# Issuing the output stores of an attention and FFN kernel from ScalarE's queue instead of SyncE's

## The chip, the cores and the metric

The kernel runs on one core of one Trainium2 chip. The metric is the device time of one execution in microseconds (us); before the change it is 480.43 us at the median of 3 runs (480.08 to 480.87). Busy times, waits and the places of single instructions come from one profiled execution, whose clock starts at the first recorded instruction.

A core has five engines, each with an instruction queue that it works off in order: TensorE (PE) multiplies matrices, VectorE (DVE) and ScalarE (ACT) work on elements, GpSimd (POOL) issues most loads here, SyncE (SP) only issues DMAs. Engines wait for one another by semaphores.

## What is computed

Attention with a projected key and value length (64 instead of 1024), for 8 batches and 8 heads, and then a feed-forward network on its result.

```python
k_proj = einsum('ks,bhsd->bhkd', E, k)             # 8 x 8 x 64 x 64
v_proj = einsum('ks,bhsd->bhkd', F, v)
attn   = softmax(q @ k_proj.T / 8)                 # q: 8 x 8 x 1024 x 64
a      = attn @ v_proj
x      = a.transpose(0, 2, 1, 3).reshape(8192, 512)
h      = x @ w_in                                  # 512 -> 2048
g      = h * (1.0 / (1.0 + exp(-1.702 * h)))
out    = g @ w_out                                 # 2048 -> 512, 8192 x 512 f32
```

All inputs are f32; the kernel multiplies in bf16 and sums in f32.

## The kernel before

**Blocks.** The 8192 tokens are taken in `NBLK` = 16 blocks of `TB` = 512, two to a batch. A block goes through these stages: scores of q and the projected k, exp, the product with the projected v, the normalization by the softmax sums, FFN1 (512 to 2048) with the activation, FFN2 (2048 to 512), and the store. From block 1 or 2 on, both FFN products are done with seven smaller products in the place of eight (a Strassen scheme, lines `u_` for FFN1 and `F` for FFN2), so that ScalarE and VectorE make sums of operands and of results beside TensorE.

**Order.** The order of the work is written out by hand. `tc.manual_schedule()` (L42) leaves every engine's queue in program order. The program is a list of words: `OPEN` (L386 to 433) for blocks 0 to about 4, `STEPS` (L434 to 445), which the loop at L777 runs for j = 4 to 12, and `TAIL` (L446 to 470). A word such as `st1@2` or `Fo0@3/A` is a step's name, the block, and at times the engine (A for ScalarE, D for VectorE) and PSUM banks; `step` (L479) issues its instructions. So an instruction moved to another engine's queue stands there where its word stands among the words that use that engine.

**Output tiles.** `o(g)` (L494 to 497) gives the block's output tile in SBUF: `o0` for the first and `o1` for the second half of the block's tokens, each 128 x 2 x 512 f32 (512 KB). The pool has one buffer for each name (`bufs=1`), so block j+1 writes to the memory from which block j is stored. Writers are `Fo0` and `Fo1` (L526 and 527, copies of a PSUM bank into the left half, on ScalarE or VectorE as the word says), and `Fd2` and `Fd1` (L528 to 531, sums on VectorE through `add` at L491). Block 0 is written by `oc` (L534).

**Stores.** The words `s0.0`, `s0.1` (block 0), `st0` and `st1` (all others) end in L547: one DMA of 512 KB from `o0` or `o1` to DRAM, issued by SyncE. The pieces of the last block at L539 and L544 are stored by SyncE too.

**What else SyncE issues.** The softmax sums of a block go `den` (L660, copies from PSUM on ScalarE or VectorE), `ga` (L266, a DMA that spreads them over the partitions), `rc` (L664, reciprocal on VectorE), `sr` (L668, a DMA to DRAM, `rdr`), `sb` (L672, two DMAs that broadcast `rdr` to all partitions, `rbc`), and `mv` (L649, VectorE multiplies the PSUM result by `rbc` into `xT`). `ga`, `sr` and `sb` are issued by SyncE. Loads of q, k and v are issued by GpSimd; `lq` (L712) waits for an `rbc` before it loads the next batch's q.

**Other names that the prediction uses.** L629 is the FFN activation into `gT`; L617, L619 and L621 are the copies `c1`, `c2`, `c3` of FFN1; L521 and L523 are the copies `Fc1`, `Fc2`, `Fc3` of FFN2; L641 is `exp`; L507 and L613 are the FFN2 and FFN1 matmuls.

Of the kernel before, what the change touches and what calls it, by code (L numbers as in the profile page):

```python
# [17 lines left out]
def kernel(ctx, tc, q, k, v, E, F,  # L18
                                                     moe_w_in, moe_w_out, out):
    nc = tc.nc  # L20
# [11 lines left out]
    NBLK = B * S // TB  # L32
# [444 lines left out]
    live, outs, tmps, rdr, uu = {}, {}, {}, {}, []  # L477

    def step(name, j, banks=(), eng=None):  # L479
# [56 lines left out]
        elif i in ("st0", "st1", "s0", "st2", "st4", "st0h"):  # L536
            ov = out[b * S:(b + 1) * S, :].rearrange("(p j) m -> p j m", j=J)[:, c * JB:(c + 1) * JB]
            if i == "st2":
                nc.sync.dma_start(out=ov[:, t:t + 1, MH:], in_=outs[j, 0][:, t:t + 1, MH:])  # L539
            elif i == "st4":  # L540
                cs = slice(MH - t * MH, DM - t * MH)
                nc.sync.dma_start(out=ov[:, 2:, cs], in_=outs[j, 1][:, :, cs])
            elif i == "st0h":
                nc.sync.dma_start(out=ov[:, :2, :MH], in_=outs[j, 0][:, :, :MH])  # L544
            else:
                g = int(i[2]) if i != "s0" else t
                nc.sync.dma_start(out=ov[:, 2 * g:2 * g + 2], in_=outs.pop((j, g)))  # L547
        elif i == "O":
            n, g = int(p[1]), t
            if g == 0:  # L550
# [41 lines left out]
        elif i[0] == "u":  # L592
# [33 lines left out]
            else:  # L626
                out_, in_ = {"g11": (gT[:, lo, TLO], live.get((A, j))), "g21": (gT[:, hi, TLO], live.get((B_, j))),
                             "g22": (gT[:, hi, THI], u2), "g12": (gT[:, lo, THI], u1)}[t]
# [140 lines left out]
    def listed(words):  # L769
        for word in words:  # L770
            name, n = word.split("@")
            n, _, eng = n.partition("/")
            n, _, banks = n.partition(":")
            step(name, int(n), [int(x) for x in banks.split(",")] if banks else (), eng or None)

    listed(OPEN)
    for j in range(4, NBLK - 3):  # L777
        for word in STEPS:
            name, _, n = word.replace("-", "+-").partition("+")
            if due(name, j + int(n or 0)):  # L780
                step(name, j + int(n or 0))
# [31 lines left out]
```

## Time and profile before

| | us |
|---|---|
| median of 3 runs | 480.43 |
| the profiled execution, its own time | 481.29 |
| its span (first to last recorded instruction) | 479.5 |
| PE busy | 471.6 (98%) |
| DVE busy | 347.9 (73%) |
| ACT busy | 325.1 (68%) |
| POOL busy | 81.2 (17%) |
| a store, from DMA to landing, smallest, median, largest | 1.9, 3.5, 9.7 |

A row of a timeline has the start in us, the time that the row's instructions took together, the engine (SPq is SyncE's queue of DMA issues), the line of the kernel, the operation, output and input, and how many instructions there are in the row; in brackets stands how long the engine had been idle before it and who ended that. All PSUM banks are called `k_ps`, and `u1_sb` and `u2_sb` appear as `u_sb`, `o0_sb` and `o1_sb` as `o_sb`. "us to landing" of a DMA is the time from its issue to the last byte's semaphore. A row of the windows has the busy time of PE, PE's weight loads, DVE, ACT and POOL in a stretch, then TensorE's clock as a share of full speed, the busy share of the DMA engines and what they moved in GB/s.

### The profile page before, as it was taken

The numbers are of one execution on the slowest core, as the hardware profiler recorded it, in microseconds if no ns is written. First come the engines' busy times: TensorE is split into PE (matmuls) and PEld (weight loads), VectorE is DVE, ScalarE is ACT, GpSimd is POOL, SyncE is SP. The second block draws the span as 40 slices with busy tenths as digits, with TensorE's granted clock in tenths as the row PEclk, the third lists the DMA queues.
The fourth block names the chain that finished last, engine by engine and source line by source line (L and its number), as shares of the span: only waits on it lengthen the run. The fifth ranks groups of instructions, "written<-read, shape, count | busy, mean of one in ns | idle before, by whom it ended". The sixth has DMA issues, their size and how long they took to land.

```text
span 479.5 us, 11084 instructions
## 1 busy us (share of the span) xinstructions
PE 471.6 (98%) x4613; PEld 375.7 (78%) x4621; DVE 347.9 (73%) x633; ACT 325.1 (68%) x561; POOL 81.2 (17%) x105
## 2 busy tenths in 40 slices
PE   8999999999999999999999999999999999999996
PEld 4644446887878788887888878887888888888885
DVE  4556588578687867869585895958688695959673
ACT  2665389689576867677686757868577777757452
POOL 7562116015000150004200070001400000000000
PEclk9999999999999999999999999999999999999999
DMA  9999999859913299166983299451950505132013
GB/s 163 200 188 203 195 224 140 151 150 167 224 75 90 94 149 251 43 174 43 192 211 87 93 92 235 120 134 47 116 151 23 158 3 134 48 90 89 0 46 133
DMA packets 102390, 61.43 MB, mean 128 GB/s; under 512 B 67524, under 2 KB 91588, under 8 KB 102340
## 3 DMA queue, kind: packets, MB, share of 16 engines
q0 software_dynamic: 86496, 29.37, 54.2%
q1 hardware_dynamic: 15764, 31.10, 22.0%
q8 instruction: 36, 0.59, 0.5%
q10 hardware_dynamic: 80, 0.26, 0.2%
q14 instruction: 14, 0.11, 0.1%
HBM read 72.88 MB, written 16.99 MB: 187 GB/s over the span
## 4 chain that ended last, share of the span: by engine, by line
PE 82%; DMA 11%; DVE 3%; ACT 1%; POOL 1%; issue 1%; SPq 0%; DVEq 0%; ACTq 0%; POOLq 0%
PE k_ps L507 36%; PE k_ps L613 33%; DMA w_out_sb<-in_moe_w_out_dram 3%; PE k_ps L559 3%; PE k_ps L242 2%; PE k_ps L677 2%; DMA v_sb<-in_v_dram 2%; DMA w_in_sb<-in_moe_w_in_dram 2%; DMA rbc<-rdr 2%; PE k_ps L698 2%; PE k_ps L553 2%; DMA rdr<-rc 1%; DVE xT L649 1%; DVE sg L376 1%; PE k_ps L655 1%
## 5 line engine op out<-in xcount | busy, mean ns | idle before, releaser
L492 DVE TENSOR_TENSOR q_even<-k_ps,q_even 128x512 f32<-128x512 f32 x112 | 73.9, 686 | 52.6 <-ACT q_even L619 44.1
L507 PEld LDWEIGHTS <-sg 128*128 128x128 bf16 x960 | 93.6, 98 | 11.6 <-issue 0.9
L613 PEld LDWEIGHTS <-late 128*128 128x128 bf16 x896 | 87.5, 98 | 10.3 <-issue 0.2
L613 PE MATMUL k_ps<-xw,late 128*128 128x256 bf16 x672 | 95.3, 273 | 0.0
L507 PE MATMUL k_ps<-tw,sg 128*128 128x256 bf16 x720 | 88.8, 273 | 0.0
L629 ACT ACTIVATE gT<-q_even 128x512 bf16<-128x512 f32 x112 | 67.8, 629 | 18.8 <-PE k_ps L507 13.7
L507 PEld LDWEIGHTS <-gT 128*128 128x128 bf16 x720 | 69.0, 98 | 12.5 <-issue 4.8
L629 ACT ACTIVATE gT<-k_ps 128x512 bf16<-128x512 f32 x112 | 63.0, 599 | 20.2 <-PE k_ps L613 19.8
L613 PEld LDWEIGHTS <-w_in_sb 128*128 128x128 bf16 x672 | 64.7, 98 | 12.5 <-issue 4.9
L613 PE MATMUL k_ps<-xT,w_in_sb 128*128 128x256 bf16 x448 | 66.1, 273 | 0.0
L70 POOL DMA_DIRECT2D q_sb<-in_q_dram x56 | 49.0, 908 | 79.2 <-PE k_ps L698 69.6
L507 PE MATMUL k_ps<-w_out_sb,gT 128*128 128x256 bf16 x480 | 59.6, 273 | 0.4 <-ACT k_ps L521 0.4
L376 DVE TENSOR_TENSOR sg<-gT 128x1024 bf16<-128x1024 bf16 x60 | 40.6, 683 | 0.4 <-ACT gT L629 0.4
L621 ACT COPY q_even<-k_ps 128x512 f32<-128x512 f32 x40 | 23.5, 589 | 24.3 <-PE k_ps L613 24.0
L641 ACT ACTIVATE expT<-k_ps 128x512 bf16<-128x512 f32 x60 | 32.9, 607 | 7.5 <-PE k_ps L242 7.0
L649 DVE TENSOR_TENSOR xT<-k_ps,rbc 128x512 bf16<-128x512 f32 x52 | 33.0, 682 | 0.9 <-DMA rbc<-rdr 0.8
L613 PE MATMUL k_ps<-xw,w_in_sb 128*128 128x256 bf16 x224 | 33.4, 273 | 0.0
L613 PE MATMUL k_ps<-xT,late 128*128 128x256 bf16 x224 | 33.3, 273 | 0.0
L507 PE MATMUL k_ps<-w_out_sb,sg 128*128 128x256 bf16 x240 | 31.0, 273 | 0.0
L507 PE MATMUL k_ps<-tw,gT 128*128 128x256 bf16 x240 | 29.0, 273 | 0.0
L619 ACT COPY q_even<-k_ps 128x512 f32<-128x512 f32 x36 | 21.5, 598 | 10.7 <-PE k_ps L613 10.6
L712 POOL COPY held<-rbc 1x1 f32<-1x1 f32 x5 | 0.9, 173 | 157.9 <-DMA rbc<-rdr 157.9
(129 smaller groups left out, 602.4 us busy)
## 6 DMA issues: line engine op xcount, KB each, us to landing
out_dram<-o_sb SPq DMA_DIRECT2D x31, 512.0 KB, 3.6
rbc<-rdr SPq DMA_DIRECT2D x26, 512.0 KB, 6.8
k_sb<-in_k_dram POOLq DMA_DIRECT2D x7, 1024.0 KB, 10.8
q_sb<-in_q_dram POOLq DMA_DIRECT2D x56, 128.0 KB, 4.4
v_sb<-in_v_dram POOLq DMA_DIRECT2D x7, 1024.0 KB, 18.5
w_in_sb<-in_moe_w_in_dram POOLq DMA_DIRECT2D x8, 256.0 KB, 10.6
w_out_sb<-in_moe_w_out_dram POOLq DMA_DIRECT2D x4, 512.0 KB, 12.1
v_sb<-in_v_dram POOLq DMA_DIRECT2D x4, 256.0 KB, 10.7
```

The source lines that it names most:

```text
L70: nc.gpsimd.dma_start(out=qt[b][:, j], in_=qv[:, j])
L242: nc.tensor.matmul(outs[i][r.start + c:r.start + c + w], lhsTs[i][ri, c:c + w], rhss[i][ri], start=True, stop=True)
L376: nc.vector.tensor_tensor(t[i - 1], in0, in1, op=ALU.add if i == 1 else ALU.subtract)
L492: nc.vector.tensor_tensor(out_, in0, in1, op=ALU.add)
L507: nc.tensor.matmul(dst, x[:, k_, t * P:(t + 1) * P], w[:, k_], start=(first and k_ == 0), stop=(final and k_ == FH - 1), skip_group_check= ...
L559: nc.tensor.matmul(h_ps, w_in_sb[:, kc, t * P:(t + 1) * P], xT[j][:, kc, :], start=(kc == 0), stop=(kc == KC - 1))
L613: nc.tensor.matmul(live[h, j][:, r], a[:, k_, f:f + P], w[:, k_], start=(i in (1, 5) and r == 0 and k_ == 0), stop=(i in (2, 3, 4) and r = ...
L619: copy(u1, live[B_, j])
L621: copy(u2, live[G, j])
L629: nc.scalar.activation(out_, in_, AF.Gelu_apprx_sigmoid)
L641: nc.scalar.activation(expT[j][:, 2 * n + t, :], live[f"S{n}{t}", j], AF.Exp, scale=scale)
L649: nc.vector.tensor_tensor(x_of(j)[:, n, :], live[f"V{p[1]}{t}", j], rbc[j][:, n, :], op=ALU.mult)
```

## The change

The DMA at L547 is issued by ScalarE for blocks 0 to 13, and by SyncE as before for blocks 14 and 15.

```diff
             else:
                 g = int(i[2]) if i != "s0" else t
-                nc.sync.dma_start(out=ov[:, 2 * g:2 * g + 2], in_=outs.pop((j, g)))
+                (nc.scalar if j < NBLK - 2 else nc.sync).dma_start(out=ov[:, 2 * g:2 * g + 2], in_=outs.pop((j, g)))
```

This moves 28 DMAs of 512 KB from SyncE's queue to ScalarE's. SyncE is left with 59 DMAs of 87. ScalarE's queue gets the 28 DMAs and 10 instructions that wait for semaphores on their behalf. The queues of TensorE, VectorE and GpSimd keep their instructions and their order. The word lists are the same in both kernels, so on ScalarE each store stands after the ScalarE instruction whose word comes before it: for example, `st0@2` after `Fc2@3` and ahead of `Fo0@3`, which writes `o0`, and `st1@2` after `u0.c1@4`.

## The prediction

> **What bounds the kernel.** I read the page first: busy times, the chain that ended last, the DMA issues.
>
> ```profile
> PE 471.6 (98%) x4613; PEld 375.7 (78%) x4621; DVE 347.9 (73%) x633; ACT 325.1 (68%) x561; POOL 81.2 (17%) x105
> ...
> PE 82%; DMA 11%; DVE 3%; ACT 1%; POOL 1%; issue 1%; SPq 0%; DVEq 0%; ACTq 0%; POOLq 0%
> ...
> out_dram<-o_sb SPq DMA_DIRECT2D x31, 512.0 KB, 3.6
> rbc<-rdr SPq DMA_DIRECT2D x26, 512.0 KB, 6.8
> ```
>
> TensorE is busy 98% of the span; the DMA share of the chain is the opening loads and the broadcasts `rbc`. TensorE's waits add up to about 3.3 us in the whole run, most before 80 us. The only one in the blocks concerned is this:
>
> ```profile
> PE k_ps L507 <- ACT k_ps L521: 0.4, 1, 0.4
> ```
>
> So nothing waits for a store, or for SyncE, and there is almost nothing to win. And since TensorE is full from 80 us to the last 15 us, a delay that reaches it is not made up later. The question is only what delays reach it. For this I listed SyncE's own timeline (each row two DMAs) against ScalarE's at the places where the word list puts the stores.
>
> ```profile
> 124.92 3.89 SPq L547 DMA_DIRECT2D out_dram<-o_sb  x2
> ...
> 180.65 1.26 SPq L672 DMA_DIRECT2D rbc<-rdr  x2
> 182.00 3.47 SPq L547 DMA_DIRECT2D out_dram<-o_sb  x2
> ...
> 209.44 3.83 SPq L547 DMA_DIRECT2D out_dram<-o_sb  x2
> ```
>
> SyncE has nothing else to do, so a store leaves as soon as its tile is written: block 2's at 124.92 and 128.47. On ScalarE it leaves when the word list gets there, perhaps 18 us later. `o0` and `o1` have one buffer each, so the next block's writers wait for its landing.
>
> **What the Trainium skill says.** "DMA: Bandwidth & Descriptors", section "Issuing engines are not separate DMA queues": DMAs of all issuers run on the same 16 engines and interleave; issuing elsewhere saves only sequencer time. The same page, "Queues, rings and completion order": SP and ACT each own one ring on each engine, which alternates between its rings by packets. The trace agrees for the queues it shows: between 185 and 187 us packets of `rbc` and of GpSimd's loads ran with shares of 0.56 and 0.56. So a store in ACT's ring no longer stands behind `rbc` in SP's ring but beside it. "Perfetto Trace Analysis", section "DMA Instruction — HWDGE (DVE, Sync)": the sequencer waits for the DMA's semaphores and is free when descriptors are pushed; the data movement lies outside the recorded span. The trace agrees: a store's row lasts 338 ns at the median, its landing takes 3.5. ScalarE's only DMA row (L80, 560 ns, against 593 for SyncE's first) makes an issue equally dear on both.
>
> **Part 1: the issue itself on ScalarE, steady blocks 5 to 13 (18 stores).** In the steady order `st0` stands after the second `L629` of the row at 211.55 and `st1` after the first of 216.57.
>
> ```profile
> 211.55 1.15 ACT L629 ACTIVATE gT<-q_even 128x512 bf16<-128x512 f32 x2 [1.40 <-PE k_ps L507]
> 212.70 0.58 ACT L621 COPY q_even<-k_ps 128x512 f32<-128x512 f32 x1
> ...
> 216.57 1.08 ACT L629 ACTIVATE gT<-k_ps 128x512 bf16<-128x512 f32 x2 [0.57 <-PE k_ps L613]
> 217.54 0.63 ACT L629 ACTIVATE gT<-q_even 128x512 bf16<-128x512 f32 x1
> 218.28 0.58 ACT L660 COPY den<-k_ps 128x512 f32<-128x512 f32 x1
> ```
>
> Both tiles were written before (SyncE stored them at 209.44 and 212.92), so the DMA waits for nothing. In the trace, ScalarE's semaphore events fire about 0.05 us after the preceding instruction's wait ends, even while that still runs; so the issue (0.34 us) lies under a 0.6 us activation. For `st0` the next copy waits for TensorE until 212.60 anyway; for `st1`, `den` at 218.28 has 0.25 us to spare. Cost: 0 each. If that cover is gone, 0.34 us per store on an engine that is 68% busy, most of it absorbed. Next writers come more than 10 us later. The bounds: 0, and for an issue of 0.96 us (the longest store row) 0.3 us per block, 3 us.
>
> **Part 2: the opening list, blocks 0 to 4, whose order was drawn up with stores that cost ScalarE nothing.** Block 0 leaves at about 70 and 76 instead of 57; the next writers are at 86 and 93: 0. Block 1's `st0` keeps its time: 0. The rest by places.
>
> A: block 1's `st1` goes from 106.27 to about 117, into `rdr` and `rbc` of block 4, which landed at 133.04, 0.66 us before their use at 133.70, and ahead of the write at 123.35. A store is 128 packets of 4 KB at about 0.165 us, so 1.3 us of all 16 engines: beside 0.66 of slack, and with GpSimd's loads that much earlier, 0 to 0.8; I take 0.2.
>
> B: block 2's stores.
>
> ```profile
> 143.22 0.58 ACT L523 COPY u_sb<-k_ps 128x512 f32<-128x512 f32 x1 [2.39 <-PE k_ps L507]
> 144.66 0.61 ACT L527 COPY o_sb<-k_ps 128x512 f32<-128x512 f32 x1
> 145.13 0.64 ACT L641 ACTIVATE expT<-k_ps 128x512 bf16<-128x512 f32 x1
> 145.81 0.57 ACT L617 COPY k_ps<-k_ps 128x512 f32<-128x512 f32 x1
> 146.96 0.60 PE L613 MATMUL k_ps<-xw,late 128*128 128x256 bf16 x4
> 148.20 0.69 DVE L492 TENSOR_TENSOR o_sb<-k_ps,u_sb 128x512 f32<-128x512 f32 x1
> 149.58 1.04 PE L507 MATMUL k_ps<-tw,gT 128*128 128x256 bf16 x8
> ```
>
> `st0@2` stands behind L523, which waits for TensorE until 143.18: issue at 143.24. The quickest 512 KB store in a quiet stretch (264 to 270 us) landed after 2.6 us, and here the DMA share is 0.06: landing 145.85. But L527 writes the same `o0` at 144.66: ScalarE stands for 1.2 us. Behind it are `exp` and the bank copy L617, which then ends near 147.6 instead of 146.38; TensorE at 146.96 had 0.58 to spare, so it is 0.7 late. `st1@2` stands behind L617, leaves at about 147.1 and lands at 149.7; DVE's add at 148.20 waits 1.5, TensorE at 149.58 had 0.69 to spare: 0.85 late in all, not on top. I take 0.9. With landing in 1.9 us (the quickest seen, for 128 KB) it is 0; with 3.5, the median, both steps grow by 0.9: 2.7.
>
> C: block 3's two stores leave back to back behind the L629 at 161.58. Two issues put `den` at 162.07 back by 0.35 to 0.7; the L521 behind it had 0.36 to spare, TensorE 0.12 more: 0.15 (0 to 0.3).
>
> D: block 4's stores leave at about 184.0 and 188.9.
>
> ```profile
> 192.00 2.48 DVE L649 TENSOR_TENSOR xT<-k_ps,rbc 128x512 bf16<-128x512 f32 x4 [0.82 <-DMA rbc<-rdr]
> 194.60 1.03 PE L507 MATMUL k_ps<-w_out_sb,gT 128*128 128x256 bf16 x8 [0.36 <-ACT k_ps L521]
> ```
>
> ```profile
> 184.00:190.00 6.00, 6.00 (x60) 5.19 (x57) 4.61 (x8) 4.76 (x10) 0.00 (x0) 1.00 1.12 247
> ```
>
> Here DMA is full (share 1.12) with `rbc` and GpSimd's loads. Before, these stores followed `rbc` in SyncE's ring and took 9.7 us to land; `rbc` landed at 191.9 and DVE was already waiting for it; TensorE follows through L521 with 0.05 to spare. Beside `rbc` in a ring of their own, two stores take 1.3 us of all engines each, one or both of it ahead of `rbc`'s end: 1.3 to 2.0. Part of that may come out of GpSimd's share: 0.5 at least. I take 1.35.
>
> **Sum.** 0 + 0.2 + 0.9 + 0.15 + 1.35 + 0.1 for the odd steady issue = 2.7 us. The profiled execution took 481.29 (span 479.5, 1.8 around it), 0.86 above the median of 480.43; 481.3 + 2.7 = 484.0, and on the median 483.1. SyncE's lighter queue gives nothing: of its `ga`, `sr`, `sb` one stood behind stores, by 0.33 us and with some 5 us of slack.
>
> **Rivals.** Measurement tells 0.2%, about 1 us, from no change: 479.5 to 481.4 is "same".
> R1, ScalarE's stall at B is not passed on, as its waiting instructions are taken in another order than I read: only A, C, D remain, 1.7 us: 482.1. Against it: the events fire in order. 0.13.
> R2, an issue costs ScalarE about 1 us each time: 3 us in the steady blocks and 1 more at C: 487. For it: 959 ns is seen on SyncE; against it: the median of 338. 0.18.
> R3, the other side, not slower: stores land faster than the old ring let them. Place: the waits of L527 at 144.66 and L649 at 192.00. From a landing of 1.9 us down, B costs nothing, and if `st0@4` is mostly through before `rbc`'s packets begin at 184.5, D costs nothing: A and C are left, 0.3, 480.7. Against it: the 2.6 in quiet. 0.13.
> Gain by some new order of transfers: 0.05, as TensorE has no idle time to give back. The forecast: 0.51.
>
> **How the numbers follow.** Slower is forecast, R1 and R2, 0.82; same R3, 0.13; faster 0.05. Low ends of A to D give 1.0 (481.4), high ends 5.8 (486.2); the range 481.2 to 486.9 holds the forecast, R1 and R2 nearly to its 487, and leaves out R3 and a gain.
>
> **What would show it.** In the changed profile: an idle of 1.2 us before L527 near 145, put down to the store; a DVE wait before the add near 149; a wait for `rbc` near 192 grown from 0.82 to above 2; TensorE's idle time up by 2 to 3 us in 140 to 200 and by nothing after 200. I am wrong if TensorE idles in steady blocks (R2), or nowhere more than before (R3).

## The result, and the profile after

The changed kernel took 483.74 us at the median of 4 runs (483.38 to 484.71), the kernel before 480.65 us at the median of 4 (the three runs known before and one more). The ratio is 1.0061, with a 95% interval of 1.0045 to 1.0077: 2.9 us (2.2 to 3.7) slower. The profiled execution took 484.71 us, with a span of 482.8.

The page of the changed kernel, the lines that answer to those of before:

```profile
PE 472.7 (98%) x4621; PEld 376.1 (78%) x4621; DVE 347.5 (72%) x633; ACT 325.4 (67%) x561; POOL 81.2 (17%) x105
...
PE 72%; DMA 19%; DVE 5%; ACT 1%; issue 1%; POOL 1%; SPq 0%; DVEq 0%; ACTq 0%; POOLq 0%
...
out_dram<-o_sb ACTq DMA_DIRECT2D x28, 512.0 KB, 2.7
rbc<-rdr SPq DMA_DIRECT2D x26, 512.0 KB, 6.9
...
out_dram<-o_sb SPq DMA_DIRECT2D x3, 512.0 KB, 2.6
```

The engines' busy times are nearly the same (TensorE's 472.7 us instead of 471.6); stores even land sooner at the median (2.7 us instead of 3.6). DMA's share of the chain is 19% instead of 11%. That share alone proves little: in the second profile of the unchanged kernel, before_again below, it is 2%. What is waited for is seen in the waits. TensorE's waits in the changed kernel (what it waited for, us in all, times, longest):

```profile
PE k_ps L185 <- DMA k_sb<-in_k_dram: 1.3, 1, 1.3
PE k_ps L688 <- DVE q_even L492: 0.9, 1, 0.9
...
PE k_ps L613 <- ACT k_ps L617: 0.5, 1, 0.5
PE k_ps L507 <- ACT k_ps L521: 0.3, 1, 0.3
```

The first is in the opening, at about 10 us, before the first store. It says nothing of the change: the second profile of the unchanged kernel, below, has it too, with 1.8 us. The second and third are new and lie at 137 and 150 us. The chain of waits leads back from the second to a DMA (start, us, what):

```profile
118.00 7.39 DMA rdr<-rc
...
126.15 9.96 DMA rbc<-rdr
...
136.23 0.69 DVE xT L649
136.92 0.61 DVE q_even L492
...
137.58 0.40 PE k_ps L688 x4
```

SyncE's small DMA to `rdr` took 7.4 us to land; before, the same one took 5.3 (116.89 to 122.16), and `rbc` left behind it at 122.28:

```profile
116.89 0.33 SPq L668 DMA_DIRECT2D rdr<-rc  x1
122.28 1.27 SPq L672 DMA_DIRECT2D rbc<-rdr  x2
```

In the changed kernel, ScalarE's timeline has a store just ahead of it:

```profile
117.42 0.34 ACTq L547 DMA_DIRECT2D out_dram<-o_sb  x1
```

This is `st1@1`, place A of the prediction. It is the reason: in the three profiles with this store here on ScalarE, `rdr` took 7.2 to 7.4 us, in the ten without a store beside it 5.1 to 5.9. Place B, in the timeline of the changed kernel:

```profile
145.67 0.59 ACT L523 COPY u_sb<-k_ps 128x512 f32<-128x512 f32 x1 [2.50 <-PE k_ps L507]
145.68 0.34 ACTq L547 DMA_DIRECT2D out_dram<-o_sb  x1
...
148.32 0.59 ACT L527 COPY o_sb<-k_ps 128x512 f32<-128x512 f32 x1 [1.08 <-DMA out_dram<-o_sb]
...
149.44 0.57 ACT L617 COPY k_ps<-k_ps 128x512 f32<-128x512 f32 x1
149.45 0.34 ACTq L547 DMA_DIRECT2D out_dram<-o_sb  x1
...
150.06 0.60 PE L613 MATMUL k_ps<-xw,late 128*128 128x256 bf16 x4 [0.49 <-ACT k_ps L617]
...
152.21 0.69 DVE L492 TENSOR_TENSOR o_sb<-k_ps,u_sb 128x512 f32<-128x512 f32 x1 [1.65 <-DMA out_dram<-o_sb]
```

It can be read straight down: the store leaves when L523's wait for TensorE ends, L527 stands until it has landed 2.6 us later, L617 follows late, TensorE waits 0.49, the second store leaves behind L617, and VectorE stands for it for 1.65.

Place D, in VectorE's timeline, is the surprise. The wait for `rbc` should have grown from 0.82 to above 2; it is 0.71:

```profile
195.26 2.48 DVE L649 TENSOR_TENSOR xT<-k_ps,rbc 128x512 bf16<-128x512 f32 x4 [0.71 <-DMA rbc<-rdr]
```

**Where the time went.** All kernels here have the same 4621 weight loads on TensorE in the same order, so the time from one of them to another can be compared between two profiles. The table gives by how much each stretch grew against the first profile of before (us; the bounds are places in that profile's time; SP or ACT says who issued block 4's stores):

| kernel | 0-60 | 112-131 | 131-141 | 141-156 | 156-178 | 178-200 | 200-300 | D's issuer |
|---|---|---|---|---|---|---|---|---|
| changed kernel | +1.10 | +0.29 | +1.05 | +0.92 | 0.00 | -0.11 | +0.03 | ACT |
| act_b1 | -0.02 | +0.74 | +0.69 | 0.00 | 0.00 | -0.68 | 0.00 | SP |
| act_b2 | +0.28 | 0.00 | 0.00 | +0.92 | 0.00 | +0.08 | 0.00 | SP |
| act_b4 | +1.04 | 0.00 | 0.00 | 0.00 | 0.00 | +0.08 | +0.11 | ACT |
| act_steady | -0.44 | 0.00 | 0.00 | 0.00 | 0.00 | -0.43 | +0.11 | SP |
| act_bufs2 | +0.03 | 0.00 | +0.92 | 0.00 | 0.00 | +0.16 | 0.00 | ACT |
| act_moved | +0.91 | 0.00 | +1.41 | 0.00 | 0.00 | -0.18 | 0.00 | ACT |
| sp_late_b1 | -0.14 | +1.35 | 0.00 | 0.00 | 0.00 | -0.68 | 0.00 | SP |
| act_b4_early | +1.58 | 0.00 | 0.00 | 0.00 | 0.00 | +0.19 | +0.11 | ACT |
| act_placed | -0.09 | 0.00 | 0.00 | 0.00 | 0.00 | +0.09 | +0.03 | ACT |
| act_placed_d | -0.68 | 0.00 | 0.00 | 0.00 | 0.00 | -0.68 | 0.00 | ACT, after `rbc` |
| before_again | +0.58 | 0.00 | 0.00 | 0.00 | 0.00 | -0.68 | 0.00 | SP |

Outside the opening and the stretch from 178 to 200 a stretch either repeats to 0.01 us or shows a wait that can be named. Those two vary by themselves, and so hide effects of their own size in a single profile.

### The profile page after: what moved, and what is told of

The parts are those of the page before. It is cut to its first block, busy times and chain, and to the rows that moved or that the text cites. A ratio compares the mean times of both kernels' runs of the same rounds, so it can differ in the third digit from the quotient of the medians.

```text
span 482.8 us, 11089 instructions
## 1 busy us (share of the span) xinstructions
PE 472.7 (98%) x4621; PEld 376.1 (78%) x4621; DVE 347.5 (72%) x633; ACT 325.4 (67%) x561; POOL 81.2 (17%) x105
## 4 chain that ended last, share of the span: by engine, by line
PE 72%; DMA 19%; DVE 5%; ACT 1%; issue 1%; POOL 1%; SPq 0%; DVEq 0%; ACTq 0%; POOLq 0%
PE k_ps L507 33%; PE k_ps L613 30%; DMA v_sb<-in_v_dram 6%; DMA rbc<-rdr 4%; DMA rdr<-rc 3%; DMA w_out_sb<-in_moe_w_out_dram 2%; PE k_ps L242 2%; DMA w_in_sb<-in_moe_w_in_dram 2%; PE k_ps L559 2%; PE k_ps L677 2%; PE k_ps L698 2%; DVE sg L376 2%; DVE xT L649 1%; DMA out_dram<-o_sb 1%; PE k_ps L655 1%
## 5 line engine op out<-in xcount | busy, mean ns | idle before, releaser
L492 DVE TENSOR_TENSOR q_even<-k_ps,q_even 128x512 f32<-128x512 f32 x112 | 73.9, 686 | 52.9 <-ACT q_even L619 44.4
L613 PEld LDWEIGHTS <-late 128*128 128x128 bf16 x896 | 87.5, 98 | 11.3 <-issue 1.2
L629 ACT ACTIVATE gT<-q_even 128x512 bf16<-128x512 f32 x112 | 67.9, 629 | 19.7 <-PE k_ps L507 13.6
L629 ACT ACTIVATE gT<-k_ps 128x512 bf16<-128x512 f32 x112 | 63.0, 598 | 19.9 <-PE k_ps L613 19.5
L619 ACT COPY q_even<-k_ps 128x512 f32<-128x512 f32 x36 | 21.5, 598 | 11.0 <-PE k_ps L613 10.9
L492 DVE TENSOR_TENSOR o_sb<-k_ps,u_sb 128x512 f32<-128x512 f32 (+1 forms) x31 | 19.7, 666 | 11.5 <-PE k_ps L507 7.9
## 6 DMA issues: line engine op xcount, KB each, us to landing
k_sb<-in_k_dram POOLq DMA_DIRECT2D x7, 1024.0 KB, 12.1
```

The costliest lines, as they stand in the source:

```text
L492: nc.vector.tensor_tensor(out_, in0, in1, op=ALU.add)
L613: nc.tensor.matmul(live[h, j][:, r], a[:, k_, f:f + P], w[:, k_], start=(i in (1, 5) and r == 0 and k_ == 0), stop=(i in (2, 3, 4) and r = ...
L619: copy(u1, live[B_, j])
L629: nc.scalar.activation(out_, in_, AF.Gelu_apprx_sigmoid)
```

## The experiments

Times are differences to the kernel before of the same group of runs, worked out from the ratio (480.6 to 480.8 us times the ratio and its 95% interval).

### One place at a time

Each of these is the kernel before with one group of stores on ScalarE:

```diff
-                nc.sync.dma_start(
+                (nc.scalar if (j, g) == (1, 1) else nc.sync).dma_start(     # act_b1
+                (nc.scalar if j == 2 else nc.sync).dma_start(               # act_b2
+                (nc.scalar if j == 4 else nc.sync).dma_start(               # act_b4
+                (nc.scalar if 5 <= j < NBLK - 2 else nc.sync).dma_start(    # act_steady
```

**act_b1.** 

> Of all stores only block 1's second (st1@1) is issued by ScalarE, at its old word. Theory (the loss comes from a few places where the word is late): rdr and rbc of block 4 are late by the store's packets, VectorE waits about 1.2 us for rbc near 135 and TensorE loses 1.0 to 1.3 us: the run is 1.1 us slower than before. The prediction on record had 0.2 (0 to 0.8) for this place. Rival (each of the 28 moved stores costs about the same on ScalarE, 3.1/28 = 0.11 us): 0.1 us slower, nothing to be seen at 135.

Measured: 1.0027 (1.0016 to 1.0038), 1.3 us slower. The size is near the one expected, but only half of it came by the way expected. VectorE's add L492 starts 1.2 us late (124.56 instead of 123.35), since it writes `o1`, which the late store still reads; that costs TensorE 0.74 and was not expected. Then `rbc` is awaited for 0.79, which costs 0.69. Before:

```profile
123.35 1.51 DVE L492 TENSOR_TENSOR o_sb<-k_ps,u_sb 128x512 f32<-128x512 f32 x2 [2.35 <-PE k_ps L507]
...
133.70 0.69 DVE L649 TENSOR_TENSOR xT<-k_ps,rbc 128x512 bf16<-128x512 f32 x1
```

In act_b1:

```profile
124.56 1.29 DVE L492 TENSOR_TENSOR o_sb<-k_ps,u_sb 128x512 f32<-128x512 f32 x2 [3.58 <-PE k_ps L613]
...
135.19 0.69 DVE L649 TENSOR_TENSOR xT<-k_ps,rbc 128x512 bf16<-128x512 f32 x1 [0.79 <-DMA rbc<-rdr]
```

The wait before L492 is put down to TensorE, but it was 2.35 us with the same TensorE work before; the surplus is the store's landing, as sp_late_b1 below shows by name. One store costs more than a third of the whole loss; an equal share for every store is ruled out.

**act_b2.** 

> Only block 2's two stores are issued by ScalarE. Theory: L527 waits 1.1 us for the landing of st0@2, L492 waits 1.6 us for st1@2, TensorE loses 0.5 and then 0.3 to 0.4: 0.9 us slower than before. Rival (same cost for each store): 0.2 us slower, in no place in particular.

Measured: 1.0028 (1.0016 to 1.0039), 1.3 us slower; in the profile 0.92 between 141 and 156 and the same waits of 1.09 (L527) and 1.65 (L492) as in the changed kernel. As the theory had it.

**act_b4.** 

> Only block 4's two stores are issued by ScalarE. The prediction on record: rbc of block 6 lands 1.3 us later, VectorE's wait at 192 grows from 0.8 to about 2.1, 1.35 us slower. Theory after the trace of the changed kernel: rbc is not late (the store's packets start near 4 us after its issue, when rbc is half done, and rdr may come earlier): 0 to 0.3 us slower. Same cost for each store: 0.2.

Measured: 1.0031 (1.0020 to 1.0041), 1.5 us slower, near the number on record. But the profile doesn't show it there: VectorE's wait for `rbc` is 0.90, the stretch grew by 0.08, and 1.04 of the profiled execution's surplus is in the opening, before any store. So neither expectation was settled by this run; see act_b4_early, before_again and act_placed_d.

**act_steady.** 

> Only the 18 stores of blocks 5 to 13 are issued by ScalarE. Theory: hidden under running activations, no place where a wait ends later: 0 (up to 0.2) us. Rival (same cost for each store): 18 x 0.11 = 2.0 us slower; an issue of nearly 1 us on ScalarE would give 3.

Measured: 1.0007 (0.9996 to 1.0017), 0.3 us (-0.2 to 0.8) slower. In ScalarE's timeline the issue lies inside an activation, and the next one starts as it would have:

```profile
215.71 0.60 ACT L629 ACTIVATE gT<-k_ps 128x512 bf16<-128x512 f32 x1 [0.56 <-PE k_ps L613]
215.77 0.34 ACTq L547 DMA_DIRECT2D out_dram<-o_sb  x1
216.20 0.59 ACT L629 ACTIVATE gT<-k_ps 128x512 bf16<-128x512 f32 x1
```

18 of the 28 stores are free or nearly so.

### How long the cover lasts

The cover of an issue is the instruction that runs on ScalarE meanwhile.

**act_steady4.** The same 18 stores, each in four DMAs:

```diff
-                nc.sync.dma_start(out=ov[:, 2 * g:2 * g + 2], in_=outs.pop((j, g)))
+                o_, d_ = outs.pop((j, g)), ov[:, 2 * g:2 * g + 2]
+                for r in range(0, P, 32 if 5 <= j < NBLK - 2 else P):
+                    n = 32 if 5 <= j < NBLK - 2 else P
+                    (nc.scalar if 5 <= j < NBLK - 2 else nc.sync).dma_start(out=d_[r:r + n], in_=o_[r:r + n])
```

> Only the stores of blocks 5 to 13 are on ScalarE, each cut into four DMAs of 32 partitions: 72 issues instead of 18, about 1.0 us of sequencer time for each store beyond one issue. Theory (issues lie under running activations as long as the cover lasts; den at 218.28 had 0.25 us to spare): st0 is hidden, st1 puts den and what follows back by up to 0.8 us, of which little reaches TensorE: 0 to 1.5 us slower than before. Rival (an issue costs ScalarE's stream its time each time): 54 x 0.34 = 18 us of ScalarE, 3 us or more slower.

Measured: 1.0239 (1.0224 to 1.0254), 11.5 us slower: my expectation was far off, the rival's direction right. The four issues of one store at 216 us (in this kernel L632 is the L629 of the others, L550 the store):

```profile
216.01 0.60 ACT L632 ACTIVATE gT<-k_ps 128x512 bf16<-128x512 f32 x1 [0.39 <-PE k_ps L616]
216.08 1.75 ACTq L550 DMA_DIRECT2D out_dram<-o_sb  x4
...
217.87 0.60 ACT L632 ACTIVATE gT<-k_ps 128x512 bf16<-128x512 f32 x1 [1.26 <-DMA out_dram<-o_sb]
...
218.52 0.41 PE L242 MATMUL k_ps<-expT,vq 64*32 64x512 bf16 x8 [0.68 <-ACT gT L632]
```

The four issues take 0.44 us each on the average, one after the other, and the activation behind them stands for 1.26 us (in act_steady it started 0.49 us after the one before it, here 1.86). It has no wait of its own and starts when the last issue ends, at 217.8; the brackets name the store because the issues wait for semaphores of earlier DMAs, but these had landed by 208.6. The late activation holds up TensorE (`PE k_ps L242 <- ACT gT L632`, 6.5 us in 8 waits over the run, and 1.2 us for ScalarE's L624). Between 60 and 200 us TensorE lost nothing against the first profile of before; it lost 4.3 us from 200 to 300 and 7.0 after that, where these stores are. So the issues are in ScalarE's stream and in order; they are free only as long as they are shorter than the instruction that runs above them. The same four-part stores on SyncE were not run, so that they cost something by themselves is not excluded; 3.6 of the 11.3 us that the profile grew there are not named by a wait of TensorE.

### Why the places cost: the buffer, lateness, or the ring

**act_bufs2.** The changed kernel with two buffers for each output tile:

```diff
-                outs[j, g] = work.tile([P, 2, DM], F32, name=f"o{g}_sb", bufs=1)
+                outs[j, g] = work.tile([P, 2, DM], F32, name=f"o{g}_sb", bufs=2)
```

> As the changed kernel, but o0 and o1 have two buffers each, so that a block's writers wait for the store of two blocks before and not of one. Theory: the waits of L527 and L492 for block 2's stores near 146 and 150 are gone, and with them about 1.0 us; block 1's late store still delays rbc of block 4 (0.9 to 1.2): 2.1 us slower than before instead of 3.1. Rival (the loss is DMA contention or issue time alone, the single buffer plays no part): as the changed kernel, 3.1 us slower.

Measured: 1.0033 (1.0024 to 1.0042), 1.6 us slower, against 2.9 for the changed kernel. In the table 141 to 156 and 112 to 131 are back to 0.00, and only 131 to 141, the wait for `rbc`, keeps its 0.92 (`rdr` took 7.2 us here too). So B, and the smaller part of A, is the wait of a writer for its single buffer; the larger part of A is not.

**sp_late_b1.** All stores on SyncE; only the order of two of its DMAs is exchanged:

```diff
-  rc@4 st1@1
+  rc@4 sr@4 st1@1
...
-  u3.P5@3:1 sr@4 u3.c1@3:3/D
+  u3.P5@3:1 u3.c1@3:3/D
```

> All stores on SyncE as before, but sr@4 is ahead of st1@1 in its queue, so that block 1's second store leaves at about 117.2 instead of 106.3. Theory (lateness alone costs: the store's packets meet GpSimd's loads and block 4's rbc): rbc lands 1 us late or more, TensorE loses 0.7 to 1.3 us: 1.0 us slower. Rival (it takes the second ring, ACT's beside SP's): 0, nothing at 135.

Measured: 1.0023 (1.0015 to 1.0030), 1.1 us slower. The size is as expected, the way was another: not `rbc`, which is awaited nowhere, but the buffer alone.

```profile
125.07 1.29 DVE L492 TENSOR_TENSOR o_sb<-k_ps,u_sb 128x512 f32<-128x512 f32 x2 [4.20 <-DMA out_dram<-o_sb]
```

The store left at 117.15 and needed 7.8 us to land, so L492 stood 1.85 us longer than before (4.20 instead of 2.35), and TensorE lost 1.35. That makes everything later, and `rbc` (landed at 134.38, before 133.04) is then in time. A late store costs without ScalarE too.

**act_moved.** The changed kernel, with three words moved to where their tiles are ready:

```diff
-  ... rc@4 st1@1 ...              +  ... u2.c1@2:7/A st1@1 ...
-  ... Fc2@3/A st0@2 ...           +  ... u0.g11@3 st0@2 ...
-  ... u0.c1@4:4/A st1@2 ...       +  ... u1.g12@3 st1@2 ...
```

> As the changed kernel, but three words of the opening list are moved to where their tile is ready: st1@1 behind u2.c1@2, st0@2 behind u0.g11@3, st1@2 behind u1.g12@3. Theory (what costs is the late place in ScalarE's queue, not the queue): places A and B cost nothing, C 0.1 and D 0 to 1.3 remain: 0.1 to 1.5 us slower, with TensorE's idle time between 100 and 160 us as before. Rival (ScalarE's queue or ring itself costs): 2 to 3 us slower.

Measured: 1.0025 (1.0016 to 1.0034), 1.2 us slower. B is gone (0.00). But TensorE's idle time between 131 and 141 is not as before: the stretch grew by 1.41, more than in the changed kernel. Here the theory of lateness alone fell. The timeline shows what was overlooked:

```profile
123.58 1.25 SPq L672 DMA_DIRECT2D rbc<-rdr  x2
126.05 0.34 ACTq L547 DMA_DIRECT2D out_dram<-o_sb  x1
129.40 0.34 ACTq L547 DMA_DIRECT2D out_dram<-o_sb  x1
...
136.11 0.69 DVE L649 TENSOR_TENSOR xT<-k_ps,rbc 128x512 bf16<-128x512 f32 x1 [1.51 <-DMA rbc<-rdr]
```

On SyncE these two stores left at 124.92 and 128.47, hardly sooner, but in the same queue behind `rbc`, which landed 10.1 us after its second issue. From ScalarE's queue they go beside it, and it takes 11.8. That is the mechanism that the prediction had for D, found at block 4's `rbc` (the section "Queues, rings and completion order" of the Trainium skill's page "DMA: Bandwidth & Descriptors" says that the two queues have rings of their own, between which an engine alternates). The trace agrees: between 131 and 133 us 134 packets of SyncE's queue and 112 of ScalarE's ran. SyncE's order had been a priority that nobody wrote down.

**act_placed.** As the changed kernel, `st1@1` as in act_moved, and block 2's stores after the landing of `rbc`, yet well ahead of the next writer:

```diff
-  ... u2.P4@3 mv.0.0@4 u2.d2@3 ...
+  ... u2.P4@3 mv.0.0@4 st0@2 st1@2 u2.d2@3 ...
```

> As the changed kernel, but st1@1 goes behind u2.c1@2 (about 98 us, as in the run with three moved words), and st0@2 and st1@2 go behind mv.0.0@4, where rbc of block 4 has just landed (about 134.5): after the broadcast and still 10 us ahead of the next writer. Theory (a store costs where its packets meet an rbc that is awaited, or where a writer waits for it, and nowhere else): no wait for rbc near 135, none for a store near 145; TensorE full from 80 to 190; 0.2 to 0.8 us slower than before, for C, D and the steady stores. Rival (ScalarE's queue costs in itself): as with the three words moved, 1.2 us slower.

Measured: 1.0017 (1.0010 to 1.0024), 0.8 us slower. All stretches from 60 to 178 are back to 0.00, with the stores on ScalarE: nothing waits for `rbc`, which the stores now follow. It landed 10.0 us after its second issue, with no store near it. In the kernel before it took 10.1 with both stores behind it on its queue, so these had cost it nothing.

```profile
133.61 0.69 DVE L649 TENSOR_TENSOR xT<-k_ps,rbc 128x512 bf16<-128x512 f32 x1
133.91 0.82 ACTq L547 DMA_DIRECT2D out_dram<-o_sb  x2
```

### Block 4's stores

**act_b4_early.**

```diff
+    b4 = [w for w in STEPS if w != "st0"]
+    b4.insert(b4.index("u2.c1+1") + 1, "st0")
...
-        for word in STEPS:
+        for word in (b4 if j == 4 else STEPS):
```

together with ScalarE as the issuer for j = 4 alone. 

> Only block 4's two stores on ScalarE, st0@4 moved forward behind u2.c1@5, so that it leaves at about 182.0 (as on SyncE) instead of 184.0, and its packets fall into the middle of rbc's. Theory (two rings share the engines, rbc pays for the store's packets): VectorE's wait for rbc near 192 grows by 0.6 to 1.3 us beyond that with the word in its place; 1 to 2 us slower. Rival (the store takes its time from GpSimd's loads or idle slots, rbc is not late): the wait stays near 0.8, 0 to 0.3 us slower.

Measured: 1.0017 (1.0010 to 1.0024), 0.8 us slower; the wait for `rbc`:

```profile
193.76 2.48 DVE L649 TENSOR_TENSOR xT<-k_ps,rbc 128x512 bf16<-128x512 f32 x4 [1.01 <-DMA rbc<-rdr]
```

Neither a growth by 0.6 and more, nor 0 to 0.3 us in time. But `rbc` did pay for the store: it landed 11.7 us after its second issue, against 11.0 in act_b4. It had left 0.5 us sooner, measured against TensorE's work, and so the wait hardly grew (0.90 in act_b4, 1.01 here).

**before_again.** The kernel before, unchanged. 

> The kernel before, unchanged, for a second profile of it: how far do its opening (loads up to 60 us) and its wait for rbc near 192 differ from one execution to the next? Expected: ratio 1.000; the opening within 1 us of the first profile; the wait for rbc between 0 and 1 us.

Measured: 1.0004 (0.9992 to 1.0016). The opening was 0.58 us longer than in the first profile, and the wait near 192 was not there at all:

```profile
191.88 2.48 DVE L649 TENSOR_TENSOR xT<-k_ps,rbc 128x512 bf16<-128x512 f32 x4
```

So the 0.82 us that the prediction started from are a chance of the first execution. Of the profiles with block 4's stores on SyncE, sp_late_b1, act_b1, before_again and act_steady4 have no wait there, act_steady has 0.39, act_b2 0.90 and the first one 0.82. With those stores on ScalarE in or near their old place, all six profiles have it (0.64 to 1.01). In TensorE's time a stretch without the wait is 0.68 shorter.

The traces show why it comes and goes. With block 4's stores on SyncE, `rbc` landed 10.4 to 10.6 us after its second issue in all seven profiles. But it left at times up to 1.4 us apart, measured against TensorE's work, because the `rdr` ahead of it took 5.7 to 7.0 us. With the stores on ScalarE in or near their old place, `rbc` took 10.9 to 11.7 us, 0.8 more on the average. In the changed kernel it took 11.4 (second issue at 183.74, landing at 195.14), but `rdr` had been quick and it left 0.9 us sooner than in the first profile, so that the wait there did not grow:

```profile
183.11 1.24 SPq L672 DMA_DIRECT2D rbc<-rdr  x2
```

**act_placed_d.** As act_placed, and block 4's stores moved to where `rbc` of block 6 has all but landed (in the profile they leave at 189.83 and 190.20, and it lands at 190.50):

```diff
+    b4 = [w for w in STEPS if w not in ("st0", "st1")] + ["st0", "st1"]
...
-        for word in STEPS:
+        for word in (b4 if j == 4 else STEPS):
```

> As the one before, and block 4's two stores are moved to the end of their round of the steady list, where rbc of block 6 has landed (about 192.4). Theory of the traces so far (D costs next to nothing): within 0.3 us of the one before. The prediction on record (D costs 1.35): 1.3 us faster than the one before.

Measured: 1.0005 (0.9997 to 1.0013), 0.25 us slower than before, so 0.55 faster than act_placed (0.66 between the medians, 480.73 and 481.39). The profile has no wait for `rbc` near 192, and `rbc` took 10.5 us. All 28 stores are on ScalarE here, and the loss is gone to within what can be measured. D thus costs 0.5 to 0.7 us. This version doesn't beat the kernel before.

## Why the prediction was right, point by point

The time (483.1 forecast, 483.74 measured), the sign and the mechanism held: TensorE full, no gain from SyncE, losses only at named places of the opening list. The terms of the sum, however, were off in both directions: A was 1.1 us too small, D 0.8 and C 0.15 too large. That the total came within 0.2 us of the measured loss is in good part luck.

Of the signs that the prediction named, the two waits at B came, and nothing grew after 200 us (0.03). Two did not come: the wait for `rbc` near 192 stayed at 0.71, and TensorE lost 0.8 us from 141 to 200, not 2 to 3; 1.34 was lost before that, at A. One sum is wrong, too: the low ends of A to D add up to 0.5, not to the 1.0 named there, so that the prediction's own lowest case, 480.9, lies under its range.

| term | taken (range) | shown |
|---|---|---|
| steady stores | 0 | 0.3 (-0.2 to 0.8) by time, 0.1 at most in profiles |
| A, `st1@1` | 0.2 (0 to 0.8) | 1.34 in the changed kernel (0.29 + 1.05), 1.43 alone |
| B, block 2 | 0.9 (0 to 2.7) | 0.92 |
| C, block 3 | 0.15 (0 to 0.3) | 0.00 |
| D, block 4 | 1.35 (0.5 to 2.0) | 0.55 by time; 0 against the first profile, 0.5 to 0.9 against profiles without the wait |

The shown terms add up to about 2.8 us (1.34 + 0.92 + 0.55), the measured loss is 2.9.

**Steady stores.** Right: act_steady. What stood there as the cost without cover, "0.34 us per store ... most of it absorbed", was too mild: act_steady4, whose issues outlast the cover, lost 11.5 us for 54 more issues, 0.21 us each, about half of an issue of 0.44 us.

**A** was under-sized. The step that failed is "beside 0.66 of slack, and with GpSimd's loads that much earlier". The store's cost fell on `rdr` alone and was larger than the 1.3 us of its packets: `rdr` was 2.1 us longer on its way (7.4 instead of 5.3), while `rbc` behind it then took as long as before (9.96 us instead of 10.10). Of the 2.0 us by which `rbc` thus landed late, 0.66 was slack and 0.29 TensorE had already lost; about 1.0 is left, and 1.05 was lost. GpSimd's loads gave nothing back (the k load at the time landed after 12.1 us instead of 10.4). I had seen the write of `o1` at 123.35 and gave it no price, though 117 plus a landing of 7 us (the store at 128.47 took 7.0) reaches it. act_bufs2 parts the two: with a second buffer only the 0.92 of the late `rbc` is left.

**B** was right in every step: the wait of L527 1.08 (1.2 forecast), TensorE's first loss 0.49 (0.7), the wait of L492 1.65 (1.5), 0.92 in all (0.85 to 0.9). The quiet landing time of 2.6 us, read from another stretch, was measured as 2.62. act_bufs2 shows that it is the buffer.

**C** costs nothing: `den` is put back by 0.38 us, within the 0.35 to 0.7 forecast, but L521 behind it by only 0.04, and TensorE's stretch from 156 to 178 repeats to 0.00.

**D** was over-sized, though its mechanism held: a store beside `rbc` makes `rbc` longer, by 0.8 us on the average (10.9 to 11.7 us instead of 10.4 to 10.6) and not by the 1.3 of its packets. In the changed kernel the first packets of `st0@4` ran near 191.0, 3.6 us after its issue at 187.36, when more than half of `rbc` had passed; I had let them start at once. Where it left 2 us sooner (act_b4_early), `rbc` took 11.7, nearly the full 1.3 more. And the wait of 0.82 that the added time was to lengthen was itself a chance, which reading one profile more closely wouldn't have shown: `rbc` leaves sooner or later from one execution to the next, and with SyncE as the issuer the wait was absent in four of seven profiles. So part of the 0.8 falls into slack. What moving the stores does is to make the wait always there, some 0.5 us of TensorE's time on the average. The 1.5 us of act_b4 is more than anything else shows for the same stores (0.8 in act_b4_early, 0.55 between the last two kernels); whether the opening, which varies by 2.3 us between the profiles, makes up the rest wasn't shown.

**Rivals.** R1 fell with B. R2, an issue of near 1 us, fell: issues in the changed kernel took 338 ns at the median, 444 at most. R3 fell, as the stores landed in 2.6 us at B; its picture of faster stores was true at the median of the page, and of no use, since no one waits for the median store.

## What to carry to other kernels

A DMA that is moved to a compute engine's queue leaves when that engine's program gets there, so look not at what the issue costs (here 0.34 us, hidden under the running instruction) but at who writes the buffer next and which awaited transfer runs at the new time. A queue's order can be a priority: behind the broadcast on one queue two stores delayed nobody, beside it on another they cost 1.4 us. And where a wait varies from one execution to the next, take a second profile before building a cost on it.

## What the runs showed of the hardware that was not expected

Four DMA issues in a row on ScalarE took 1.75 us, 0.44 us each, where a single one took 0.34, and held up the next activation by 1.26 us although it had nothing else to wait for. The Trainium skill's "Perfetto Trace Analysis", section "DMA Instruction — HWDGE (DVE, Sync)", has the sequencer busy until the descriptors are generated and its semaphores pushed; the trace agrees (the activation starts at 217.87, the last issue ends at 217.82), and shows that a compute engine's next instruction waits for it. Two of act_steady4's 72 issues took 1.4 and 1.5 us; why isn't known.

The same small write to DRAM (`rdr`, 16 KB) took 1.4 us to land at 204 us, with the DMA engines nearly idle (share 0.08), 5.1 to 5.9 us at 117 us, while GpSimd's loads ran, and 7.2 to 7.4 us with a 512 KB store of another queue beside it as well. And a 512 KB store in the queue behind a broadcast did not make it longer (10.1 us, and 10.0 without), while in another queue beside it two of them did (11.8).
